# One-core attention and ReGLU kernel: first batch's chain reordered, second exponential behind a narrow FFN group, pause before the third batch cut from three steps to one

## The chip, the cores and the metric

One core of one Trainium2 chip. The metric is the device time of one launch in microseconds (us), the median of several runs. The profile is one execution, taken by the hardware profiler. Engine names as in its lines: PE is TensorE, PEld its weight loads, DVE VectorE, ACT ScalarE, POOL GpSimd, SP SyncE; a q behind the name (SPq) is the engine's sequencer, which issues DMAs. The granted clock is the share of TensorE's full clock that the profile records as granted.

## The reference, cut to what matters

```python
# q, k, v: (8 batches, 8 heads, 576 rows, 64); beacon_k, beacon_v: 16 more rows of k and v
scores = scale * q @ concat(beacon_k, k).T        # causal on k, beacons always seen
a = exp(scores - max) ; a /= a.sum(-1) + 1e-9
x = (a @ concat(beacon_v, v))                     # -> (4608 tokens, 512)
out = (relu(x @ w_gate) * (x @ w_val)) @ w_out    # 512 -> 1536 -> 512
```

## The kernel before: the parts that the change and the argument touch

The order of every engine's instructions is the order of the calls: nothing is rescheduled. Attention runs in "bursts": one pair of heads and one half of a batch's rows (g = 0: 368 rows, g = 1: 208). The FFN is a list of pieces: `up` groups for 368 tokens (wide, 1.25 us of PE) or 208 (narrow, 0.72 us), and `down` groups for 128 output rows (2.6 us in the program's own budget). A cast turns loaded float32 into bf16, a "turn" transposes one pair's q and k, a mask sets to zero what a row must not see. In the profile's lines cs, c are cast q and k, kq their transposes, s scores, p exponentials, vx values, x the attention's output, xT its transpose, hT the FFN's hidden values.

```python
s_ps: 2 score tiles; f_ps: ring of 4 PSUM banks for all else; psb = Ring("psb", 6)   # exponentials

def softmax(u):                        # two slabs a burst
    for i, (segs, cols, m) in enumerate(SLABS[u.g]):
        p = psb.tile(...); A.activation(p, u.s[i], AF.Exp, scale=scale); u.p.append(p)
def mask(u, pool=False): ...           # DVE multiply, or POOL selects
def av(u): ...                         # value product on PE, reciprocal and multiply on DVE -> x
def x_turn(u): ...                     # SyncE: DMA transposes of x into xT (batches 1 to 7)
def x_turn_pair(u, cp): ...            # the same on PE, for the first batch
def pair_turn(c, b, p, part, cps): ... # PE transposes of one pair's k and q, two copies

# head (first batch, g = 0), cut
scores(g0[0]); mask(g0[0], True)
chunk(0, 512)                          # first 512 columns of both up weights, on POOL's queue
vl[0][0].cast(G); vl[0][1].cast(G); direct(c0, 0, 0, NP, 1); vl[0][2].issue(...)
chunk(512, 1024); vl[0][2].cast(G); chunk(1024, 1536) ...
scores(g0[1]); pair_turn(c0, 0, 2, 0, VV); mask(g0[1])
scores(g0[2]); pair_turn(c0, 0, 3, 0, VV); mask(g0[2]); scores(g0[3]); av(g0[0]) ...

# steady loop, cut
T0, GAP = 8, 3
ticks = bursts[8:16] + [None] * GAP + bursts[16:] + [None]
begin = {b: T0 + GAP + 8 * (b - 1) for b in range(2, B)}
for s, u in enumerate(ticks, T0):
    ...
    if u: scores(u)                    # score products and both exponentials
    if prev:
        av(prev)
        if prev.last: x_turn(prev)     # SyncE's queue
    # jobs of this step: casts (POOL) and transposes of q and k (SyncE's queue)
    if pieces and s >= begin[pieces[0][0]] - 10:
        b, x = pieces.pop(0); x.issue()          # one load a step, SyncE's queue
        jobs.append((s + 2, cast)); jobs.append((s + 3, turn))
    if u: mask(u)
    want += budget(s)
    while ffn and ready[ffn[0][2]] <= s and spent + ffn[0][0] / 2 <= want:
        next_ffn()                     # down pieces end with a store, SyncE's queue
```

## Time and profile before

| | before |
|---|---|
| median of 3 runs | 391.31 us (389.74 to 394.99) |
| profiled span | 391.9 us |
| PE busy | 363.1 us, 93% |
| PE idle, 0 to 20 us / 90 to 126 us | 10.2 / 6.1 us |

The busy share says which engine bounds; the idle time by stage says where there is something to win; the waits by releaser say what ends the idle time. The lines are in the prediction.

### The profile page before, as it was taken

To read this page: it belongs to the slowest core of one execution; us is meant where nothing else is said; L and a number is where in the kernel's file an instruction comes from. 1 tells how busy PE (TensorE), PEld (TensorE's weight loads), DVE (VectorE), ACT (ScalarE), POOL (GpSimd) and SP (SyncE) were. 2 spreads that over 40 slices of the span, in tenths; PEclk is the share of its full clock that TensorE was granted. 3 is DMA by queue.
4 is the path that set the end of the run, shared out by engine and by line. 5 is a ranking of instruction groups with operands and counts; after the bars stand their busy time and mean duration, and the time that the engine had idled before them with its cause. 6 is when DMAs were issued, how large, how long until landed. Compare 5 with 4: busy or idle time off the path is not lost.

```text
span 391.9 us, 9542 instructions
## 1 busy us (share of the span) xinstructions
PE 363.1 (93%) x3727; PEld 235.9 (60%) x3745; DVE 189.0 (48%) x644; ACT 204.0 (52%) x369; POOL 72.2 (18%) x90
## 2 busy tenths in 40 slices
PE   3689989997995999999999999999999999999994
PEld 1456666666653667566477646865487646865762
DVE  2847366545522577256345543566165543552220
ACT  5565267635544555555466545665366554642321
POOL 6616033021231223012212221022212000000000
PEclk9999999999998999999999999999999999999999
DMA  8999997697897997588779497777775113001202
GB/s 161 169 159 164 206 229 147 145 181 133 173 204 176 147 205 134 129 186 166 166 151 177 87 212 174 121 139 158 164 145 95 23 45 90 15 8 43 82 30 85
DMA packets 157795, 53.12 MB, mean 136 GB/s; under 512 B 146480, under 2 KB 153136, under 8 KB 157744
## 3 DMA queue, kind: packets, MB, share of 16 engines
q1 hardware_dynamic: 149840, 45.37, 58.0%
q0 software_dynamic: 7760, 6.88, 11.2%
q8 instruction: 31, 0.51, 0.6%
q14 instruction: 20, 0.16, 0.2%
q10 hardware_dynamic: 144, 0.20, 0.2%
HBM read 38.47 MB, written 9.44 MB: 122 GB/s over the span
## 4 chain that ended last, share of the span: by engine, by line
PE 83%; DMA 7%; ACT 3%; POOL 2%; SPq 2%; issue 2%; DVE 1%; ACTq 0%; DVEq 0%; POOLq 0%
PE f L416 23%; PE f L410 23%; PE f L432 22%; PE f L377 8%; PE s L339 6%; DMA stg<-in_v_dram 5%; ACT p L346 2%; DMA xT<-x 1%; DMA stg<-in_beacon_k_dram 1%; POOL vx L269 1%; ACT ob L435 1%; SPq L393 1%; DVE hT L424 0%; SPq L436 0%; PE f L322 0%
## 5 line engine op out<-in xcount | busy, mean ns | idle before, releaser
L424 DVE TENSOR_TENSOR hT<-g,f 128x208 bf16<-128x208 f32 (+14 forms) x288 | 92.2, 351 | 86.0 <-PE f L416 55.1
L410 PE MATMUL f<-xT,wg 128*128 128x368 bf16 (+1 forms) x768 | 126.7, 287 | 7.0 <-DMA xT<-x 6.0
L416 PE MATMUL f<-xT,wv 128*128 128x368 bf16 (+1 forms) x768 | 126.2, 287 | 2.2 <-DVE hT L424 2.2
L413 ACT ACTIVATE g<-f 128x368 f32<-128x368 f32 (+1 forms) x192 | 78.4, 413 | 84.2 <-PE f L410 41.6
L346 ACT ACTIVATE p<-s 128x992 bf16<-128x992 f32 (+2 forms) x128 | 103.7, 864 | 21.9 <-PE s L339 19.2
L432 PE MATMUL f<-wo,hT 128*128 128x512 bf16 x414 | 95.4, 379 | 0.9
L416 PEld LDWEIGHTS <-wv 128*128 128x128 bf16 x768 | 71.4, 98 | 28.1 <-DVE hT L424 2.9
L410 PEld LDWEIGHTS <-wg 128*128 128x128 bf16 x768 | 70.0, 99 | 28.2 <-DMA xT<-x 6.4
L432 PEld LDWEIGHTS <-hT 128*128 128x128 bf16 x432 | 41.2, 98 | 46.3
L282 POOL CAST c<-stg 128x1024 bf16<-128x1024 f32 (+1 forms) x30 | 32.1, 1069 | 158.6 <-DMA stg<-in_q_dram 158.6
L435 ACT COPY ob<-f 128x512 f32<-128x512 f32 x36 | 21.1, 585 | 70.1 <-PE f L432 61.5
L385 DVE RECIPROCAL rall<-f 128x2 f32<-128x2 f32 (+1 forms) x96 | 16.7, 174 | 77.7 <-PE f L377 77.2
L377 PEld LDWEIGHTS <-p 128*128 128x128 bf16 (+2 forms) x960 | 36.9, 107 | 14.5 <-issue 12.3
L377 PE MATMUL f<-vx,p 128*128 128x65 bf16 (+2 forms) x960 | 43.9, 200 | 1.2 <-POOL vx L267 0.7
L357 DVE TENSOR_TENSOR p<-p,tri 128x160 bf16<-128x160 bf16 (+1 forms) x126 | 41.0, 353 | 8.2 <-ACT p L346 7.9
L339 PE MATMUL s<-kq 64*128 64x208 bf16 (+4 forms) x512 | 35.3, 259 | 5.3 <-DVE kq L325 4.1
L386 DVE TENSOR_TENSOR x<-f,rall 128x128 bf16<-128x128 f32 (+1 forms) x96 | 36.3, 379 | 3.5
L339 PEld LDWEIGHTS <-kq 64*128 64x128 bf16 x512 | 16.6, 96 | 22.5 <-issue 18.1
L269 POOL CAST vx<-stg 128x1024 bf16<-128x1024 f32 (+2 forms) x22 | 20.1, 921 | 52.0 <-DMA stg<-in_v_dram 26.5
L325 DVE COPY kq<-f 128x192 bf16<-128x192 bf16 (+2 forms) x19 | 9.1, 519 | 3.9 <-PE f L322 3.2
L319 PE MATMUL f<-ident,c 64*128 64x64 bf16 x12 | 0.5, 236 | 5.7 <-ACT c L279 5.7
L322 PE MATMUL f<-ident,cs 64*64 64x64 bf16 x264 | 4.9, 208 | 0.6 <-DVE hT L424 0.5
(45 smaller groups left out, 42.5 us busy)
## 6 DMA issues: line engine op xcount, KB each, us to landing
out_dram<-ob SPq DMA_DIRECT2D x36, 256.0 KB, 3.2
stg<-in_v_dram SPq DMA_DIRECT2D x24, 256.0 KB, 5.0
stg<-in_k_dram SPq DMA_DIRECT2D x18, 256.0 KB, 3.6
stg<-in_q_dram SPq DMA_DIRECT2D x18, 256.0 KB, 4.1
stg<-in_v_dram SPq DMA_DIRECT2D x8, 224.0 KB, 3.7
wg<-in_moe_w_gate_dram POOLq DMA_DIRECT2D x3, 512.0 KB, 5.7
wv<-in_moe_w_val_dram POOLq DMA_DIRECT2D x3, 512.0 KB, 8.2
wo<-in_moe_w_out_dram POOLq DMA_DIRECT2D x3, 512.0 KB, 11.3
```

The source lines that it names most:

```text
L282: cp(self.c[:n], self.st[:n])
L339: T.matmul(s[:, a, c:c + n], kq[rows, 0, u.pi, kt * P:(kt + 1) * P], kq[rows, 1, u.pi, Nb + q0:Nb + q0 + n], start=True, stop=True)
L346: A.activation(p[:, :, :cols], u.s[i][:, :, :cols], AF.Exp, scale=scale)
L357: V.tensor_mul(p[:, :, :m], p[:, :, :m], tri[:, :, :m])
L377: T.matmul(o[:m, j, a, 0:D + 1], p[:kr, a, c:c + m], vs[u.b % 2][:kr, kt, 2 * u.pi + a, 0:D + 1], start=first, stop=(kt == kts[-1]), skip_ ...
L386: V.tensor_mul(u.x[:m, i0:i0 + j1 - j0, u.pi * P:(u.pi + 1) * P].rearrange("p j (a d) -> p j a d", a=2), o[:m, j0:j1, :, 0:D], r.unsqueeze ...
L410: T.matmul(g[:, :mn], wg[:, ki, nf * P:(nf + 1) * P], xT[:, ki, m0:m0 + mn], start=(ki == 0), stop=(ki == KM - 1))
L413: A.activation(gs[:, :mn], g[:, :mn], AF.Relu)
L416: T.matmul(u[:, :mn], wv[:, ki, nf * P:(nf + 1) * P], xT[:, ki, m0:m0 + mn], start=(ki == 0), stop=(ki == KM - 1))
L424: V.tensor_mul(hbs[i][:, nf, c - i * HB:e - i * HB], gs[:, c - m0:e - m0], u[:, c - m0:e - m0])
L432: T.matmul(o, hbs[i][:, nf, ms * P:(ms + 1) * P], wo[:, nf, :], start=(nf == 0), stop=(nf == NF - 1))
L435: A.copy(ob, o)
```

## The change

Its intent: start the FFN earlier, never let PE run out of work around the third batch, and keep two long exponentials from standing ahead of a small FFN group. Cut to its core:

```diff
-    psb = Ring("psb", 6)
+    psb = Ring("psb", 8)
-    NA, PRE = 3, 16
+    NA, PRE = 2, 16                    # FFN groups ahead of the first batch's second half
-        mask(g0[0], True)
-        chunk(0, 512)
-        vl[0][0].cast(G)
-        vl[0][1].cast(G)
+        mask(g0[0], True, (0,))
+        chunk(0, 256)
+        mask(g0[0], True, (1,))
+        pair_turn(c0, 0, 2, 0, VV)
+        scores(g0[1])
+        vl[0][0].cast(G)
+        mask(g0[1], which=(0,))
+        pair_turn(c0, 0, 3, 0, VV)
+        scores(g0[2])
+        mask(g0[1], which=(1,))
+        vl[0][1].cast(V)
+        scores(g0[3])
+        mask(g0[2])
+        av(g0[0])
         direct(c0, 0, 0, NP, 1)
         vl[0][2].issue(lambda ap: G.memset(ap, 0.0))
+        mask(g0[3], True)
+        chunk(256, 512)
+        ...                            # value products and transposes of the four pairs
         while len(ffn) > LEFT:
+            if len(ffn) == LEFT + 1:   # ahead of the last down group
+                bk[1].turn(V.tensor_copy)
+                pair_turn(c1, 1, 0, 2, VA)
             next_ffn()
-        T0, GAP = 8, 3
+        T0, GAP = 8, 1
+                late = not turn and ffn and ready[ffn[0][2]] <= s and ffn[0][0] < 1
+                start(u); qk(u)
+                softmax(u, (0,) if late else (0, 1))
+            if late:                   # run behind the first and the second FFN piece of the step
+                rest = [lambda: (softmax(u, (1,)), mask(u, which=(0,))), lambda: mask(u, which=(1,))]
```

Output stores also get a queue variable, which names SyncE's queue in both cases and changes nothing.

More of the change, by code (lines that the diff above doesn't have):

```diff
@@ L341, in qk, with softmax @@
             u.s.append(s)
-    def softmax(u):
-        for i, (segs, cols, m) in enumerate(SLABS[u.g]):
+    def softmax(u, which=(0, 1)):
+        for i in which:
+            cols = SLABS[u.g][i][1]
             p = psb.tile([P, 2, 512], BF16, name="p")
@@ L347, in softmax, with mask @@
             u.p.append(p)
-    def mask(u, pool=False):
-        for i, (segs, cols, m) in enumerate(SLABS[u.g]):
-            p = u.p[i]
+    def mask(u, pool=False, which=(0, 1)):
+        for i in which:
+            p, m = u.p[i], SLABS[u.g][i][2]
             if pool:
@@ L435, in go @@
             A.copy(ob, o)
-            nc.sync.dma_start(out[i * HB + ms * P:i * HB + (ms + 1) * P, :], ob)
+            oq = nc.sync if len(ffn) < 8 else OQ
+            oq.dma_start(out[i * HB + ms * P:i * HB + (ms + 1) * P, :], ob)
         return go
@@ L453, in range_count @@
         V.tensor_copy(cnt, cnt_ps)
-    NA, PRE = 3, 16
+    OQ = nc.sync
+    NA, PRE = 2, 16
     tiles = []
@@ L528 @@
         bk[1].issue()
+        mask(g0[3], True)
+        chunk(256, 512)
+        av(g0[1])
+        x_turn_pair(g0[0], A.copy)
+        av(g0[2])
+        x_turn_pair(g0[1], A.copy)
+        av(g0[3])
+        for u in g0[2:]:
+            x_turn_pair(u, A.copy)
         chunk(512, 1024)
@@ L555 @@
         ffn[n0:2 * NF + 2] = ffn[2 * NF:2 * NF + 2] + ffn[n0:2 * NF]
-        scores(g0[1])
-        pair_turn(c0, 0, 2, 0, VV)
-        mask(g0[1])
-        scores(g0[2])
-        pair_turn(c0, 0, 3, 0, VV)
-        mask(g0[2])
-        scores(g0[3])
-        av(g0[0])
-        av(g0[1])
-        mask(g0[3])
-        av(g0[2])
-        x_turn_pair(g0[0], A.copy)
-        av(g0[3])
-        for u in g0[1:]:
-            x_turn_pair(u, A.copy)
         for _ in range(NA):
@@ L603 @@
                     x.cast(G)
-        bk[1].turn(V.tensor_copy)
-        pair_turn(c1, 1, 0, 2, VV)
         pieces = []
@@ L637 @@
         for s, u in enumerate(ticks, T0):
-            if u and u.b == 1 and u.g == 0 and not u.last:
+            turn = u and u.b == 1 and u.g == 0 and not u.last
+            if turn:
                 pair_turn(c1, 1, u.pi + 1, 2, VA)
+            late = False
             if u:
-                scores(u)
+                late = not turn and ffn and ready[ffn[0][2]] <= s and ffn[0][0] < 1
+                start(u)
+                qk(u)
+                softmax(u, (0,) if late else (0, 1))
             if prev:
@@ L654 @@
                         jobs.append((s + 3, lambda x=x: x.turn()))
-            if u:
+            rest = []
+            if late:
+                rest = [lambda: (softmax(u, (1,)), mask(u, which=(0,))), lambda: mask(u, which=(1,))]
+            elif u:
                 mask(u)
@@ L661 @@
                 next_ffn()
+                if rest:
+                    rest.pop(0)()
+            for f in rest:
+                f()
         while ffn:
```

## The prediction

> **What bounds the kernel now.** I read the busy table first, then busy time by stage, then whom TensorE (PE) waited for, then the timeline at each place where it stood still. PE is the bound: busy 93% of 391.9 us, against 52% for ScalarE (ACT) and 48% for VectorE (DVE). The change takes away no matmul, so it can only win PE's idle time, 391.9 - 363.1 = 28.8 us, and time in which PE ran at a lowered clock. The stages, each row the length, then PE, weight loads, DVE, ACT, POOL, clock, DMA share, GB/s:
>
> ```profile
> 0.00:20.00 20.00, 9.78 (x173) 6.69 (x174) 10.74 (x29) 10.77 (x17) 12.52 (x26) 1.00 1.04 166
> 20.00:50.00 30.00, 28.45 (x321) 18.07 (x322) 15.01 (x53) 14.30 (x26) 8.06 (x12) 1.00 1.08 179
> 50.00:60.00 10.00, 8.49 (x223) 6.47 (x222) 7.49 (x24) 6.57 (x14) 2.97 (x4) 1.00 0.96 218
> 60.00:90.00 30.00, 29.61 (x310) 19.28 (x312) 16.33 (x55) 17.76 (x31) 6.24 (x6) 1.00 0.91 155
> 90.00:126.00 36.00, 29.88 (x298) 18.97 (x299) 14.82 (x56) 18.05 (x32) 7.89 (x8) 0.95 0.87 170
> 126.00:380.00 254.00, 250.01 (x2396) 163.53 (x2409) 124.58 (x429) 134.80 (x249) 34.56 (x34) 1.00 0.59 120
> ```
>
> Idle PE: 10.2 us in the first 20, 1.6 in the next 30, 1.5 in 50 to 60, 6.1 in 90 to 126 (with a dip of the clock), 4.0 in the long steady part, 5.0 in the drain at the end. The reader should see that four fifths of what can be won lies before 126 us. PE's longest waits there:
>
> ```profile
> PE f L410 <- DMA xT<-x: 6.0, 2, 3.9
> PE f L319 <- ACT c L279: 5.7, 1, 5.7
> PE s L339 <- DVE kq L325: 4.1, 4, 1.8
> PE s L339 <- ACT p L346: 0.9, 1, 0.9
> PE f L377 <- POOL vx L267: 0.7, 1, 0.7
> ```
>
> The 5.7 us is the first load, which nothing in the diff touches. The timeline of the head shows the rest:
>
> ```profile
> 11.30 2.19 DVE L357 TENSOR_TENSOR p<-p,tri 128x480 bf16<-128x480 bf16 x2
> 11.54 1.81 POOL L269 CAST vx<-stg 128x1024 bf16<-128x1024 f32 x2
> 14.48 0.81 PE L339 MATMUL s<-kq 64*128 64x128 bf16 x6 [1.77 <-DVE kq L325]
> 16.19 1.49 ACT L346 ACTIVATE p<-s 128x992 bf16<-128x992 f32 x2 [2.62 <-PE f L377]
> 19.90 1.03 PE L410 MATMUL f<-xT,wg 128*128 128x368 bf16 x4
> ```
>
> The mask of 0.6 us took 2.19 beside POOL's casts, the next copy of q and k stood behind it, so the fourth pair's scores came at 14.48. Its exponential came only at 16.19, because the ring of six probability tiles made it wait for the first pair's value product. The FFN begins at 19.90. The third place, at 110 to 126 us, in the chain of waits:
>
> ```profile
> 115.18 0.86 SPq L436
> ...
> 116.61 1.22 SPq L393
> ...
> 117.88 1.26 SPq L393
> ...
> 119.19 2.55 DMA xT<-x
> 121.75 0.14 issue
> 121.88 1.39 PE f L410 x4
> 123.27 1.23 PE f L416 x4
> ```
>
> The transposes of the third batch's attention had their data by about 111.2, but SyncE's queue, issuing in order behind loads, stores and other transposes, sent them from 116.6 on; PE stood 3.9 us and then ran four matmuls in 1.39 and 1.23 us where 0.62 is usual.
>
> **What the Trainium skill says.** (1) "TensorE: Matmul & The Clock Gate", Part 1: after an idle window of about 3.4 us the array runs at half its clock, for about another 3.4 us of work. The trace agrees: after the 3.9 us wait eleven matmuls started about 0.154 us late each, 1.7 us, and the granted clock over 121.5 to 125.5 is 0.57. The 2.1 us wait at 90 us has no such tail. (2) "SBUF — State Buffer", "SBUF: two separate sides": VectorE and GpSimd lock a shared port for a whole instruction, and the loser blocks. The 2.19 us mask agrees, as does a 1.44 us mask at 143.44 beside a cast at 143.53. (3) "DMA: Bandwidth & Descriptors", "Issuing engines are not separate DMA queues": queues share the same 16 engines and interleave. Agrees: a value load issued at 15.19, just behind two weight chunks, landed at 28.42.
>
> **The change, part by part.**
>
> *Head.* The first weight chunk becomes 256 columns wide, the pairs' turns alternate with scores, one value cast moves to DVE, the probability ring grows to 8. Worked forward with old durations: the third pair's q lands at 8.7 as before, its turn is 0.54 on PE and 1.02 of DVE copies; scores of pair 2 at 9.2, exponentials 9.65 to 11.1. The last pair's q lands at 11.1, so its turn ends on PE at 11.4 and its copies at 12.5; exponentials of pair 3 at 11.8 to 13.3, of pair 4 at 13.3 to 14.8. POOL masks pair 4 by 15.3. Four value products of 0.8, each with 0.76 of DVE behind it, and the transposes with 0.47 ACT copies run from 13.5 to about 18.5. FFN at 18.5 instead of 19.9, less a little: **-1.5**.
>
> *20 to 50 us.* The late value tile (landed 28.42, cast, 0.88 us of PE loss at 29.13) is now loaded ahead of the second half-chunk, and its cast no longer holds the third weight chunk back: -0.9. The third and fourth FFN columns may wait a little for their own chunk, and columns 512 to 1024 still land about 28.8, as the bytes ahead of them are the same: +0.2. **-0.7**.
>
> *50 to 60 us.* The second batch's first turn moves ahead of a 2.5 us output group. Old losses there: 0.25 and 1.13 us before the scores at 51.90. -1.4. But PE then arrives 3 us sooner at values whose loads are bound by DMA (cast at 54.97, already awaited twice for 0.3 us): +0.4. **-1.0**.
>
> *Pause.* Replaying the loop's own budget for a pause of 3 and of 1: before, the FFN pieces of steps 16 to 18 all run ahead of the third batch and it is left with 12 narrow pieces and two output groups while its transposes are under way. With 1, four of the wide groups and three of those narrow pieces move to steps 17 and 18, between its bursts. SyncE has, before those transposes, one load (1.2 us) and one pair of transposes (2.5 us) fewer, and begins its loads a step earlier in an idle stretch of 3.3 us (62.8 to 66.1). Estimate: the transposes issue from 103, with the data, and land by 109.3; the FFN wants them at 112.3. This removes 2.1 + 0.3 us at 90, and 3.9 + 0.2 + 1.7 at 122: -8.2. Against it: the third batch is wanted two steps earlier, at about 81 us, with its last needed transposes landing at 80 to 82; and the second batch's transposes stand behind one more load and turn at about 64: +1.2 for both. **-7.0**.
>
> *Second exponential.* In 16 of the 58 steps it goes behind a narrow group. Four feed-forward accumulators hold two groups, 1.43 us of PE; two exponentials of 1.49 to 1.76 us in a row outlast that. Stalls of this kind in steps that are changed: 0.97, 0.93, 0.38, 0.76, 0.38 = 3.4 us. The first line's release is hT, which waits behind a mask stretched by a cast:
>
> ```profile
> 143.44 1.44 DVE L357 TENSOR_TENSOR p<-p,tri 128x480 bf16<-128x480 bf16 x2
> 143.53 1.22 POOL L282 CAST c<-stg 128x1024 bf16<-128x1024 f32 x1 [2.77 <-DMA stg<-in_q_dram]
> 145.29 0.53 PE L416 MATMUL f<-xT,wv 128*128 128x208 bf16 x4 [0.80 <-DVE hT L424]
> ```
>
> A cast that collides still stretches half a mask, so I count 60% of it: **-2.0**. The output queue variable names the same queue twice: 0.
>
> Sum: -1.5 - 0.7 - 1.0 - 7.0 - 2.0 = -12.2, from 391.3 to **379**.
>
> **Rivals.** *The wait moves to the third batch's start.* Before, its first scores at 89.89 already waited 0.18 us for transposes issued at 82.66 and 84.50 and landed at 89.28 and 89.85: SyncE was issuing without a break from 66 to 91. If it gains less than I work out, PE waits 3 to 5 us at about 81 us, perhaps with the half clock: total 383 to 386. For it: those landings took 5 to 6.6 us where 2.5 is usual. Against: the step earlier start. *The head is bound by bytes.* If transfers, busy from 10 to 52 us almost without a break, fix when weights and the second batch arrive, the gain of head and turn is given back at 50 to 58 us as a longer wait for values: total 382. Against: an idle dip of DMA at 28 to 31 us, which the earlier cast of the value tile would fill. *The split exponential is only a reordering.* DVE then does the same work with one more order constraint, and new collisions with casts appear elsewhere: 2 us lost, 381.
>
> **Range and chances.** Two rivals together make about 387, no counter-wait and a full 3.4 us make about 375. Runs of the kernel before spread over 5 us, 1.3%. So 375 to 386, eight times in ten. The 2% line is 383.5; most of the sum hangs on the pause, and half of it there would still reach the line with the rest: faster 0.77, same 0.21, slower 0.02.
>
> **What will show it.** Right: first FFN matmul at about 18.5; scores of the second batch within 0.3 us of the output group before them; no wait of PE for xT over 1 us and no clock below 0.9 around 105 to 125; PE idle in 126 to 380 about 2 us instead of 4. Wrong: a new line in which scores wait for the DMA of kq at 78 to 85 us, a value product waiting over 1 us for a cast at 50 to 56, FFN groups waiting for weights between 20 and 30, or masks as long as before with the same stalls. If the pause gives nothing, the time is near 386.

## The result, and the profile after

The changed kernel took 381.31 us (379.84 to 382.54, 4 runs) against 392.44 (389.74 to 394.99, 4 runs) of the kernel before on the same chip: ratio 0.9716, 95% interval 0.9636 to 0.9796. Ratios here are the mean time of one kernel's runs over that of the other's of the same rounds, so they are not quite the ratio of the medians quoted.

Busy time by stage, changed kernel (length, then PE, PEld, DVE, ACT, POOL, clock, DMA share, GB/s):

```profile
0.00:20.00 20.00, 10.13 (x171) 6.95 (x172) 9.51 (x28) 10.82 (x17) 14.50 (x30) 1.00 1.11 166
20.00:50.00 30.00, 29.20 (x342) 18.71 (x342) 15.81 (x55) 14.58 (x25) 8.01 (x13) 1.00 1.12 183
50.00:60.00 10.00, 9.28 (x193) 6.43 (x191) 6.18 (x21) 6.37 (x14) 3.10 (x4) 1.00 1.13 212
60.00:90.00 30.00, 29.30 (x308) 18.53 (x304) 17.31 (x55) 18.83 (x32) 8.07 (x8) 1.00 1.09 172
90.00:126.00 36.00, 36.00 (x382) 23.92 (x382) 18.65 (x66) 20.95 (x39) 7.29 (x7) 1.00 0.92 179
126.00:370.00 244.00, 243.50 (x2337) 159.38 (x2335) 121.86 (x418) 130.98 (x243) 32.50 (x33) 1.00 0.65 122
```

Idle PE is down from 6.1 to 0.0 us in 90 to 126 us and from 4.0 to 0.5 in the long part behind it (which ends 10 us sooner here). The first 20 us are as idle as before: 9.9 us against 10.2. What PE waited for, changed kernel:

```profile
PE f L319 <- ACT c L279: 5.7, 1, 5.7
PE f L322 <- DMA cs<-in_q_dram: 1.5, 2, 1.1
PE f L322 <- DMA cs<-in_k_dram: 0.9, 1, 0.9
```

The 6.0 us for xT are gone. New are waits of the turns in the head for the transfer of the last two pairs' q and k. The head's timeline, changed kernel:

```profile
12.20 0.53 PE L322 MATMUL f<-ident,cs 64*64 64x64 bf16 x22 [1.12 <-DMA cs<-in_q_dram]
14.98 1.49 ACT L347 ACTIVATE p<-s 128x992 bf16<-128x992 f32 x2 [0.20 <-PE s L339]
20.16 1.43 PE L411 MATMUL f<-xT,wg 128*128 128x368 bf16 x4
21.39 1.43 PE L417 MATMUL f<-xT,wv 128*128 128x368 bf16 x4
```

The FFN began at 20.16 us, later than the 19.90 of before, and its first groups took 1.23 us from start to start instead of 0.62: ten matmuls began 0.154 us late each, 0.307 us apart. The kernel before shows the same 0.307 us at 122.1 to 124.9 us, where its profile does record a clock of 0.5; so here too the array was at half its clock. The stage table prints 1.00 for this stretch because the profile holds no clock record before 23.38 us.

The place where the transposes of the third batch's attention were late, changed kernel, DVE finishing the data, SyncE issuing, PE using it:

```profile
106.46 0.56 DVE L387 TENSOR_TENSOR x<-f,rall 128x384 bf16<-128x384 f32 x1
106.59 1.26 SPq L438 DMA_DIRECT2D out_dram<-ob  x1
107.95 4.22 SPq L394 DMA_TRANSPOSE xT<-x  x3
116.26 0.79 PE L411 MATMUL f<-xT,wg 128*128 128x368 bf16 x4
```

The issue comes 0.9 us after the data is there (5.4 us before the change), and PE comes to need the result 9.2 us after the data is there (6.8 us before the change, when PE stood ready at 117.94 for data of 111.13).

### The profile page after: what moved, and what is told of

It reads as the page before. It is cut to its first block, busy times and chain, and to the rows that moved or that the text cites. A ratio compares the mean times of both kernels' runs of the same rounds, so it can differ in the third digit from the quotient of the medians.

```text
span 380.8 us, 9562 instructions
## 1 busy us (share of the span) xinstructions
PE 363.3 (95%) x3745; PEld 236.4 (62%) x3745; DVE 189.3 (50%) x642; ACT 204.3 (54%) x370; POOL 73.5 (19%) x94
## 4 chain that ended last, share of the span: by engine, by line
PE 89%; DMA 4%; SPq 2%; POOL 1%; ACT 1%; DVE 1%; issue 0%; POOLq 0%; ACTq 0%; DVEq 0%
PE f L411 24%; PE f L417 24%; PE f L433 23%; PE f L378 9%; PE s L339 7%; DMA cs<-in_q_dram 2%; DMA stg<-in_q_dram 1%; SPq L296 1%; DMA xT<-x 1%; POOL cs L308 1%; SPq L394 1%; ACT p L347 1%; PE f L402 0%; PE f L322 0%; ACT ob L436 0%
## 5 line engine op out<-in xcount | busy, mean ns | idle before, releaser
L347 ACT ACTIVATE p<-s 128x992 bf16<-128x992 f32 (+2 forms) x128 | 105.5, 864 | 20.0 <-PE s L339 19.8
L433 PE MATMUL f<-wo,hT 128*128 128x512 bf16 x432 | 96.8, 379 | 0.1
L358 DVE TENSOR_TENSOR p<-p,tri 128x160 bf16<-128x160 bf16 (+1 forms) x124 | 42.1, 359 | 5.0 <-ACT p L347 4.0
L269 POOL CAST vx<-stg 128x1024 bf16<-128x1024 f32 (+2 forms) x21 | 19.1, 908 | 80.0 <-DMA stg<-in_v_dram 68.9
L339 PEld LDWEIGHTS <-kq 64*128 64x128 bf16 x512 | 16.6, 96 | 18.6 <-issue 17.0
L322 PEld LDWEIGHTS <-cs 64*64 64x64 bf16 x264 | 3.8, 118 | 5.9 <-issue 2.2
```

The source lines that it names most:

```text
L339: T.matmul(s[:, a, c:c + n], kq[rows, 0, u.pi, kt * P:(kt + 1) * P], kq[rows, 1, u.pi, Nb + q0:Nb + q0 + n], start=True, stop=True)
L347: A.activation(p[:, :, :cols], u.s[i][:, :, :cols], AF.Exp, scale=scale)
L358: V.tensor_mul(p[:, :, :m], p[:, :, :m], tri[:, :, :m])
L433: T.matmul(o, hbs[i][:, nf, ms * P:(ms + 1) * P], wo[:, nf, :], start=(nf == 0), stop=(nf == NF - 1))
```

## The experiments

Edits are against the changed kernel unless the kernel before is named. Each was timed over five rounds. All gave correct results.

**The changed kernel again** (no edit).

> The changed kernel once more, unedited, as the yardstick for the other runs of this job. Its first profile: first FFN matmul at 20.16 us, its first ten FFN matmuls 0.307 us apart where 0.153 is usual, last pair's q landed at 12.16. If the half clock up to 23.4 us is chance[...], this profile may show the first FFN matmuls at full speed and about 1.5 us less up to the first output group; if the head's order makes it, it shows them slow again. Time 379.5 to 382.5.

380.59 us (380.22 to 382.05), ratio to before 0.9689 (0.9652 to 0.9726). Its profile (span 378.5 us):

```profile
11.15 0.53 PE L322 MATMUL f<-ident,cs 64*64 64x64 bf16 x22 [0.65 <-DMA cs<-in_q_dram]
18.93 1.03 PE L411 MATMUL f<-xT,wg 128*128 128x368 bf16 x4
19.80 0.78 PE L417 MATMUL f<-xT,wv 128*128 128x368 bf16 x4
```

The last pair's q landed a microsecond sooner, and the FFN matmuls ran at full speed. So neither the late landing nor the half clock belongs firmly to the kernel; both vary between executions. The first output group began at 42.70 us here, at 45.27 in the first profile.

**Pause back to three steps.**

```diff
-        T0, GAP = 8, 1
+        T0, GAP = 8, 3
```

> The changed kernel with the pause put back to three steps. Theory (the pause pays most): about 7.5 us over the changed kernel, 388 to 390, with PE waiting some 2 us for xT near 88 us and 3 to 4 us near 118, and a clock of 0.5 for 3.4 us after the second. Rival (the gain came from the split exponential and the head, and transposes are on time anyway once SyncE has less to wait for): within 2 us of the changed kernel, no wait for xT over 1 us.

388.75 us, 8.2 over the changed kernel of the same job. PE's wait for xT, this run:

```profile
PE f L411 <- DMA xT<-x: 5.6, 2, 4.2
```

The waits are back (1.4 us near 91, 4.2 near 121), and a clock of 0.5 for 3.41 us from 121.37. The rival falls: the head's and the exponentials' gains do not put SyncE in time.

**Exponentials never split.**

```diff
-                late = not turn and ffn and ready[ffn[0][2]] <= s and ffn[0][0] < 1
+                late = False
```

> The changed kernel with both exponentials always together, as before the change. Theory (the split takes 3.4 us of stalls away behind 126 us, and costs 0.6 us at one mask at 65 us): 2.5 to 3.5 us over the changed kernel, with FFN matmuls of narrow groups waiting 0.4 to 0.9 us in four to six places. Rival (a mere reordering; the stalls of before were collisions that moved with the pause): within 1 us.

383.01 us, 2.4 over the changed kernel. All that the waits view lists for PE between 126 and 360 us in this run:

```profile
PE f L411 <- ACT g L414: 0.7, 3, 0.2
```

The gain stands, slightly under the range expected, but not as its list said: the stalls of 0.97 and 0.93 us of the kernel before, behind masks stretched by casts, are not here either, nor in the profile of the pause alone below. That is not because casts and masks no longer meet: 28 masks overlap a cast in this profile, as in that of the kernel before, and one took 1.27 us at 131 us, but behind 126 us PE waits for none of them. Start against start with the three profiles of the unedited kernel, what the split removes is a delay of 0.43 us at each of three bursts and of 0.13 us at three or four others; the profiles account for 1.6 to 1.8 us behind 85 us, the timing for 2.4. The rest is not explained.

**Head of before** (old order, first chunk of 512, ring of 6, three FFN groups).

```diff
-    psb = Ring("psb", 8)
+    psb = Ring("psb", 6)
-    NA, PRE = 2, 16
+    NA, PRE = 3, 16
         (and the lines of the head as in the kernel before)
```

> The changed kernel with the head of before: first batch's chain in the old order, first weight chunk 512 wide, probability ring of 6, three FFN groups before the second half. Prediction's term: 1.5 + 0.7 us over the changed kernel. What the first profile says (first FFN matmul 0.26 us later and 1.55 us of half clock in the new head, against 0.88 us less at the value tile): between 1 us below and 0.5 above the changed kernel. First FFN matmul at 19.9.

383.44 us, 2.9 over the changed kernel: outside what I expected from the first profile, beyond the prediction's 2.2. Yet its first FFN matmul came at 19.26 us, between the changed kernel's 18.93 and 20.16. PE's waits in this run show where the head pays:

```profile
PE f L378 <- POOL vx L267: 1.3, 1, 1.3
PE f L322 <- DMA cs<-in_q_dram: 0.9, 1, 0.9
```

The first is the late value tile near 29 us. The second, at 48.7 us, is new: the second batch's turn, which the changed kernel has moved forward, finds its q not landed. In the changed kernel the weights, and all that is queued behind them, arrive about 3 us sooner (the last output weights at 42.88 us against 45.85 before), because the value tile's cast no longer holds up the third weight chunk.

**Third pair's scores ahead of the last pair's turn.**

```diff
-        pair_turn(c0, 0, 3, 0, VV)
         scores(g0[2])
         mask(g0[1], which=(1,))
+        pair_turn(c0, 0, 3, 0, VV)
```

> The changed kernel with the third pair's scores put ahead of the last pair's turn on PE. In both profiles of the changed kernel the third pair's scores stood ready (copies done at 10.2) behind the last pair's turn, which waited for q (11.15 to 12.2 us). Theory: third pair's exponentials begin near 11.3 instead of 12.3 to 13.3, the first FFN matmul comes 0.5 to 1.2 us sooner than in the changed kernel, total 0.5 to 1.2 us less. Rival (the head is bound by DVE and by the value casts, not by the exponentials): no change within 0.4 us.

380.85 us, ratio 0.9692: the same as the changed kernel. The third pair's exponentials did begin at 11.59 us, but the masks before the last pair's copies on DVE ran beside a POOL cast:

```profile
10.99 2.06 DVE L358 TENSOR_TENSOR p<-p,tri 128x480 bf16<-128x480 bf16 x2 [0.62 <-issue]
11.83 1.06 POOL L269 CAST vx<-stg 128x1024 bf16<-128x1024 f32 x1
14.04 0.81 PE L339 MATMUL s<-kq 64*128 64x128 bf16 x6 [1.73 <-DVE kq L325]
```

Two masks that take 0.6 us elsewhere took 2.06, and the last pair's scores came at 14.04. So earlier exponentials of the third pair did not help while the last pair's scores came late. It is no clean test of the order on PE, as the edit also put the second pair's second mask ahead of the last pair's copies on DVE.

**Pause alone, on the kernel before.**

```diff
-        T0, GAP = 8, 3
+        T0, GAP = 8, 1
```

> The kernel before with the pause of one step alone. Theory: 7 to 8.5 us less than before, 384 to 386, no wait of PE for xT over 1 us. Rival (the pause needs the head's lead, else the third batch's scores wait for their transposes): 2 to 5 us less, with scores waiting 3 us or more for the DMA of kq near 85 us.

385.24 us against 393.41 (median), 8.2 less; the ratio, 0.9834 (0.9778 to 0.9891), says less, 6.5, as two of the six runs took 389 and 390. No wait for xT or for kq in its profile, which is of one of the four runs at 384 to 385. Those four had a granted clock of 0.999 to 1.000, the two long ones 0.995. So in four runs of six the pause needed nothing of the rest; the other two won only 3.5 to 4.5 us, as the rival had it, and may have had such a wait and a half clock again. No profile of them was kept, so this stays open.

**Stores off SyncE's queue, on the kernel before.**

```diff
-            nc.sync.dma_start(out[...], ob)
+            (A if 8 <= len(ffn) < LEFT else nc.sync).dma_start(out[...], ob)
```

> The kernel before, pause of three, with the output stores of the loop issued from ScalarE's queue instead of SyncE's. Theory (the third batch's transposes were late because SyncE issued them in order behind two stores that themselves waited, at 114.76 and 116.14): transposes issue by 114.5 instead of 116.6, PE waits 1 to 2.5 us instead of 3.9 near 122, no half clock after it, total 3 to 4.5 us less than before. Rival (the transposes are late because the DMA engines are busy): they issue sooner but land as late, total within 1.5 us of before.

395.98 us, ratio 1.0057 (1.0010 to 1.0104): worse. The data was ready at 110.95, as before, and SyncE had no store left ahead of the transposes:

```profile
110.84 2.94 SPq L296 DMA_TRANSPOSE kq<-c  x2
113.83 0.58 SPq L254 DMA_DIRECT2D stg<-in_k_dram  x1
114.45 0.69 SPq L255 DMA_DIRECT2D stg<-in_q_dram  x1
115.25 5.64 SPq L393 DMA_TRANSPOSE xT<-x  x3
122.32 1.38 PE L410 MATMUL f<-xT,wg 128*128 128x368 bf16 x4 [4.55 <-DMA xT<-x]
```

My theory in this form falls: without the stores the transposes issued 1.4 us sooner, 115.25 instead of 116.61, but the three issues took 5.64 us where they took 3.84 with the stores in the same queue, and PE started no earlier (122.32 against 121.88). What stood ahead of them still was a pair of q and k transposes and a load. "They issue sooner but land as late" is what the rival said; whether busy DMA engines stretched the three issues was not tested. Behind 126 us there are also longer waits of FFN groups for ACT, 0.68 to 0.74 us at three places where the kernel before has 0.22; ACT now also issues the stores, which is the likely cause.

**Loads one step later.**

```diff
-                if pieces and s >= begin[pieces[0][0]] - 10:
+                if pieces and s >= begin[pieces[0][0]] - 9:
```

> The changed kernel with every load of batches 3 to 8 one step later, as late relative to the second batch as before the change, so only the order of FFN work against the bursts is kept. Theory A (most of the gain is that FFN pieces move behind the third batch's first bursts): total within 1.5 us of the changed kernel, with 0 to 1.5 us of waiting for kq near 84 us. Theory B (it is the step by which the loads begin earlier): 3 us or more over the changed kernel, PE waiting for xT or kq by that much.

381.13 us, ratio 0.9692. The loop begins at step 8 and loads go one a step, so with a pause of one the edit changes no instruction. It tells nothing of theories A and B, and counts as a third timing of the changed kernel.

**Loads from the fourth batch on two steps later, on the kernel before.**

```diff
-                if pieces and s >= begin[pieces[0][0]] - 10:
+                if pieces and s >= begin[pieces[0][0]] - (10 if pieces[0][0] == 2 else 8):
```

> The kernel before, pause of three, with the loads of the fourth and later batches begun two steps later, so that two loads and one pair of transposes fewer stand in SyncE's queue ahead of the third batch's output transposes; FFN order and pause as before. Theory (the wait near 122 us is SyncE's backlog): those transposes issue at 111.5 to 113 instead of 116.6, the wait falls from 3.9 to under 1 us, no half clock, total 4 to 6 us less than before; the wait at 92 us stays. Rival (what counts is that a longer stretch of FFN work lies between data and need, which only the shorter pause gives): wait of 2.5 us or more, total within 2.5 us of before.

388.15 us, 4.9 us less than before; the ratio, 0.9894 (0.9855 to 0.9932), says 4.2. With two loads and one pair of transposes fewer ahead of them, the transposes go out with the data, and the FFN of the third batch begins at 118.15 without a wait:

```profile
110.94 0.56 DVE L386 TENSOR_TENSOR x<-f,rall 128x384 bf16<-128x384 f32 x1
111.53 4.75 SPq L393 DMA_TRANSPOSE xT<-x  x3
118.15 0.79 PE L410 MATMUL f<-xT,wg 128*128 128x368 bf16 x4
```

No half clock follows. The wait at 92 us stays, as expected, and a new one of 1.9 us appears at 128.95, where the fourth batch's scores now wait for their own later loads. This shows the wait at 122 us to come from the loads and transposes ahead in SyncE's queue: pause and FFN order are those of before here. The edit also moves those loads' bytes to later, so it does not part the queue's order from the load on the DMA engines; the order of issue in the lines above is what speaks for the queue.

**First turn of the second batch back behind the output group.**

```diff
             if len(ffn) == LEFT + 1: (the two turns taken out, and put behind the loop with VV)
```

> The changed kernel with the second batch's first turn back behind the output group. The prediction's term: 1.0 to 1.4 us over the changed kernel, PE waiting 0.9 to 1.1 us for the copies before the second batch's first scores. Rival (the time is given back at the values, which are bound by their loads): no difference over 0.4 us, PE waiting longer for the value casts in the changed kernel than here.

381.64 us, ratio 0.9700. Against 0.9689 and 0.9692 of the unedited kernel that is 0.4 us, inside the intervals. The profiles show both halves: the stretch from the first output group to the second batch's first scores is 7.46 us instead of 6.52, and the next stretch, up to the third batch's first scores, 33.45 instead of 34.01 and 34.13. In the third profile of the changed kernel (from the run with the loads one step later) it is 34.46, with a wait of 0.35 us for xT in it. So at least 0.56 of the 0.94 us is given back, but not as the rival had it: no profile of the changed kernel has a wait of PE for a value cast there. What all three do have, and this run has not, is a value product waiting for masks, 0.55, 0.40 + 0.28 and 0.26 + 0.22 us. In the first profile of the changed kernel one such mask, of 0.28 us in this run, took 0.72 beside a cast:

```profile
64.28 1.14 POOL L269 CAST vx<-stg 128x1024 bf16<-128x1024 f32 x1 [1.21 <-DMA stg<-in_v_dram]
64.84 0.72 DVE L358 TENSOR_TENSOR p<-p,tri 128x256 bf16<-128x256 bf16 x1
65.62 0.45 PE L378 MATMUL f<-vx,p 128*128 128x65 bf16 x9 [0.55 <-DVE p L358]
```

**No pause.**

```diff
-        T0, GAP = 8, 1
+        T0, GAP = 8, 0
```

> The changed kernel with no pause at all. Theory (a pause only has to cover SyncE's transposes of the third batch's q and k): in the second profile of the changed kernel those landed at 80.6 us and the scores came at 83.4; without the last pause step some 5 us of FFN work less stands before them, so PE waits 1.5 to 3 us for the DMA of kq near 79 us, and the total is 0 to 2.5 us over the changed kernel (380.5 to 383). Rival (the shorter the pause the better, because more FFN work is left between data and need): 0.5 us or more below it.

385.08 us, ratio 0.9798: 4 us worse than with one step (0.9689 in another job). The third batch's scores, this run:

```profile
80.86 0.50 PE L339 MATMUL s<-kq 64*128 64x128 bf16 x6 [3.73 <-DMA kq<-c]
82.01 1.42 PE L411 MATMUL f<-xT,wg 128*128 128x368 bf16 x4
```

The last transposes of its k and q landed at 80.72. PE stood 3.73 us and paid again in the half clock that followed (0.5 for 3.41 us). So one step is the least that covers SyncE's work for the third batch here, where the loop's first load comes at its first step either way, and the rival "the shorter, the better" falls.

**A version that beats both.** The first two value loads are held back behind the first cast, the split is not used in the step before an output group, and the range check comes three pieces earlier.

```diff
-        vl[0][0].issue(lambda ap: A.activation(ap, ones[0:1], AF.Exp))
-        vl[0][1].issue()
+        A.activation(ge[0:1, 0:1], ones[0:1], AF.Exp)
         ...
         bk[0].cast(A)
+        vl[0][0].issue(lambda ap: V.memset(ap, 0.0))
+        vl[0][1].issue()
-                late = ... and ffn[0][0] < 1
+                late = ... and ffn[0][0] < 1 and s > T0 + 3
-            if len(ffn) == 10:
+            if len(ffn) == 13:
                 range_flags()
```

> The changed kernel with three more edits: the first batch's first two value loads issued behind the first cast (so that the last pair's q lands sooner), the split exponential not in the step before the first output group (0.6 us of waiting for a mask there), and the range check's three DVE operations three pieces earlier (0.8 us of PE loss near 362). If the head hangs on the landing of the last pair's q (first FFN matmul 7.8 to 8.0 us after that turn in five profiles): first FFN matmul at 17.7 to 18.7, total 377.5 to 379. If it hangs on bytes as a whole, values then land late: first FFN unchanged at 19 to 20, total 379 to 380.

378.74 us (378.31 to 379.42), ratio 0.9642 (0.9608 to 0.9675): 14.3 us under the kernel before, about 2 under the changed one. Its head:

```profile
9.75 0.54 PE L322 MATMUL f<-ident,cs 64*64 64x64 bf16 x24
12.92 1.49 ACT L347 ACTIVATE p<-s 128x992 bf16<-128x992 f32 x2 [0.20 <-PE s L339]
18.00 1.03 PE L411 MATMUL f<-xT,wg 128*128 128x368 bf16 x4
```

The last pair's q landed at 8.65 us instead of 11 to 12, its turn waits for no transfer, and the exponentials of the four pairs follow each other with gaps of 0.20 us: now ACT sets the pace of the head up to the last pair's exponentials, which end at 14.4 us. The three edits were not run apart. The profile shows the first FFN matmul 0.9 us before the earlier of the two profiles of the changed kernel, and no wait of a value product for a mask near 62 us.

## Why the prediction was right or wrong

379 us was forecast with 375 to 386 as the range; 381.31 and, in the second job, 380.59 were measured. What each part is worth, as the cost of undoing it:

| part | predicted | measured by undoing it |
|---|---|---|
| pause | 7.0 | 8.2 |
| head and the stage up to 50 us | 1.5 + 0.7 | 2.9 |
| second exponential split | 2.0 | 2.4 |
| first turn of the second batch | 1.0 | 0.4, within noise |

The last row is from another job, by ratios. The measured column sums to 13.9, more than the 12.1 between the kernels in the first job of experiments: the parts lean on each other, as the old head together with the moved turn shows (a wait for q that neither full kernel has).

*Pause: right, and its counter-waits did not come.* Of the 8.2 us that came back with the pause of three, its profile shows 5.6 us of waits for xT and a half clock of 3.41 us, some 1.7 us lost: the terms that the sum listed. The 1.2 us set against them were not seen as such: the third batch's scores had their transposes in time, and the second batch's xT was awaited for about 0.3 us in two profiles of three. The rival named for this stage was close, though: with one step less it is what happens (3.73 us). The named cause, SyncE's in-order queue, is right; of what stood ahead in it, the stores were worth 1.4 us of delay and the q and k transposes and loads the rest. The times themselves were 4 us late (data at 107.0, wanted at 116.26, where I had 103 and 112.3) as the lead from the head was missing in the first profile; the margin held.

*Head: the step that failed is "FFN at 18.5 instead of 19.9".* It took the last pair's q at 11.1 us and a chain of 7.4 us behind it. In seven profiles with this head (the three of the changed kernel, the run with the loads one step later being the third, pause three, no split, old turn, no pause) that turn resumed at 10.99 to 12.20 us and the first FFN matmul came 7.6 to 8.3 us after it, at 18.6 to 20.2. Five profiles with the old head have it at 19.3 to 19.9. So the reordering itself did not start the FFN measurably sooner: its start follows the landing of the last q, and the version above, which lets it land sooner, starts at 18.0. That head and next stage together came near their 2.2 us is luck: of the 2.9, the second profile of the changed kernel against that of the old head shows 0.3 us at the FFN's start, some 1.4 at the value tile and 0.95 at the wait for q near 48.7 us, which the prediction did not have.

*20 to 50 us: right in mechanism, too small.* The late value tile's wait is gone, 0.7 us in the profile before (0.88 from start to start, as the prediction counts) and 1.3 in the old-head run, and weights arrive 3 us sooner. The half clock at the FFN's start was not foreseen; it costs about 1.5 us in the executions that have it.

*Split exponential: right size, wrong list.* Three of the five stalls that I counted, 0.97, 0.93 and 0.76 us, are gone in the profile of the pause alone too, and a cast still stretches masks there (1.10 us at 146.8) without PE waiting more than 0.2 us. The small ones stay without the split and go with it; they and what no profile explains (0.6 to 0.8 us) make up the 2.4. So the size is partly luck.

*First turn: won, and more than half lost again.* The 0.94 us won at once is as predicted, 0.56 to 1.01 us is lost again before the third batch. The rival "bound by loads" would show as waits of PE for value casts, and there are none; the profiles show waits for masks instead, one of them beside a cast. No run settles why they come with the earlier turn.

*Signs.* Of those that the prediction named as right, the first FFN matmul at 18.5 failed; the longest wait for xT was 0.35 us in three profiles, the recorded clock around 105 to 125 us was 1.00, and the second batch's scores followed the output group without a wait. Its "four fifths of what can be won lies before 126 us" leaves out the first load's 5.7 us and the drain's 5.0 without saying so; of the whole 28.8 us it is 19.8.

Still open: whether the new head makes the half clock at the FFN's start likelier. Four of nine profiles with this head or a variant of it had it throughout the first groups, one of five with the old head; that is too few to tell.

## What to carry to other kernels

In an in-order kernel ask of every late transfer what its issuing queue had to send ahead of it, and count those instructions per step: here moving two loads and one pair of transposes from ahead of it to behind it was worth 4 to 5 us. A filler of bound-engine work (a pause) has a best length, set by what the queue must deliver before the next stage and by what work is then left to cover the stage after it; of the lengths tried, none lost 4 us and three lost 8 against one; two was not run. And when a head is reordered, first find the transfer that the longest chain hangs on, and let that one land sooner: reordering alone left the FFN's start where it was, the earlier landing came with a start 0.9 us sooner.

## What the Trainium skill lacked or had wrong

- "TensorE: Matmul & The Clock Gate", Part 1: its idle window is borne out. Waits of 3.73 to 4.24 us were followed by a clock of 0.5 for 3.41 us, one of 4.55 us by 6.83 us of it, the waits of 1.4 to 2.1 us by none. It says that the window's phase varies between runs; here that shows up as a first FFN stretch at half clock in one profile of the same kernel (until 23.38 us) and at full clock in another (from 17.64 us), about 1.5 us. That spread, 5.7 us, is wider than one window of about 3.4 us, so the phase alone does not account for it; what else does stays open.
- No page has it: a granted clock of 1.00 in a stage of this profile can mean that no record exists. The changed kernel's stage from 20 us reads 1.00 while matmuls start 0.307 us apart instead of 0.153.
- "DMA: Bandwidth & Descriptors", "Issuing engines are not separate DMA queues", calls the sequencer's time to start a DMA usually small relative to the DMA. Here one transpose takes SyncE 1.2 to 1.3 us to issue and lands about 2.5 us after its issue began when little is queued, and what stood ahead in its queue decided when the third batch's transposes went out. Moving the stores to another queue did not help here: 395.98 against 393.41 us.
